# Token mixer and channel mixer on one core: the channel mixer's first product in seven block products in the last token group alone, that group's stores on two queues, and the third output block's halves in two PSUM banks

## Chip, core and metric

The kernel runs on one core of a Trainium2 chip. The metric is device time in microseconds (us) of one execution; lower is better. Times come from repeated executions, views of single instructions from one profiled execution. PE is TensorE (the matmul engine), PEld its weight load, DVE is VectorE, ACT is ScalarE, POOL is GpSimd, SP is SyncE, which issues the DMAs. PSUM is the memory that matmuls write, in eight banks of 512 fp32 columns; SBUF is the working memory.

## What is computed

Three layers follow one another: a linear attention over 768 tokens, a gated layer, and a mixer. The change touches only the last two lines of the mixer:

```python
B, S, d_model, d_tok, d_ch = 2, 768, 384, 256, 1536
xt = x.transpose(0, 2, 1)
h  = np.maximum(xt @ w_tok1, 0.0) @ w_tok2
u  = x + h.transpose(0, 2, 1)                    # 1536 tokens x 384
h2 = np.maximum(u @ w_ch1, 0.0) @ w_ch2          # 384 -> 1536 -> 384
return u + h2
```

## The kernel before

**Precision.** Each matrix is held as a high part in the type fp32r and a low part that is what the high one leaves of fp32. A product is three matmuls: high by high, high by low, low by high (`prod`, the lines L270 to L272). Whatever is a right operand must therefore be split: ACT makes the high part, DVE subtracts it for the low part.

**Tiling of the channel mixer.** The method `rest` runs it. The 1536 tokens are three groups (`g` = 0, 1, 2) of 512 tokens, each two halves `ONE` and `TWO` of 256 columns. The hidden width 1536 is six blocks (`k`) of 256, each two half blocks of 128; `n = 6 g + k` counts all 18 blocks. Of the 384 inputs three blocks of 128 exist (`q`), and of the 384 outputs three blocks (`ct`).

**First product, two forms.** In group 0 it is ordinary (`C1`): for each half block (`b`) three products of 512 columns into one PSUM bank, 18 matmuls of 512 columns for a block. ACT writes relu as the high part `h` and a copy `r` of one half, DVE makes the low part and the two sums `ta` and `tb` that the second product wants (`C1a`, `C1b`). In groups 1 and 2 the first two input blocks form a two by two block product that is done in seven block products instead of eight (`C1s`, seven steps `m` = 0 to 6): seven products of 256 columns and two of 512 for the third input block, 21 matmuls of 256 and 6 of 512 columns. It wants sums of the weight's blocks (`sums_of_c1`, `split_c1`) and of the input's blocks, for each group of tokens anew (`sums_of_u`, `split_u`). Its results lie scattered over three banks `x`, `y`, `z` and are put together by DVE additions (L577) into `c1`, `c2`, then go through ACT for relu and high part (`C1r`), DVE for the low part (`C1l`), and DVE for the differences `ta`, `tb` (`C1t`).

**Second product.** It is in seven block products in all groups for the first two output blocks (`C2`, q = 1 to 7); `sums_of_c2` and `split_c2` make its weight sums on POOL and ACT. The third output block is ordinary (`C2d`, once for each half `t`). A C2 or C2d step is issued once for each of the 18 blocks and accumulates over the six `k` of its group in five PSUM banks (`total(g, i)`): bank 3 uses only its half `ONE`, bank 4 holds both halves of the third output block.

**Finish.** After a group's last block its sums are put together with the residual (`residual`, POOL, three a group, into the one output tile `o`), by ten steps (`finish`, m = 0 to 9, on DVE with ACT and POOL) and two `finish_rest` (L702) for the third output block. Six stores of 128 x 256 go out through SP's queue (`store`).

**Order.** Every engine executes its instructions in the order in which the program issues them. The order of the steps is written by hand as one string, `REST`: each letter or digit is one step for its next block. `a` and `b` are C1, `c` and `d` C1a and C1b, `e`, `f`, `t`, `u` the splits of `ta` and `tb`, `g` to `m` the seven steps of C1s, `o` to `s` C1r, C1l and C1t, `1` to `7` C2, `8` and `9` C2d, `A`, `B` sums and splits of the second product's weights, `C`, `D` those of the first's, `E`, `F` those of the input, `G` to `P` finish, `Q`, `S` finish_rest, `R` residual, `z` a check of the fast path's range (its flag is one small matmul) and `Z` the reading of its flag. The eight banks are shared out as five for `total` and three for everything else.

Of the kernel before, what the change touches and what calls it, by code (L numbers as in the profile page):

```python
# [13 lines left out]
ALU = mybir.AluOpType  # L14
# [3 lines left out]
B, H, S, D = 2, 8, 768, 48  # L18
E = H * D
P = 128  # L20
# [3 lines left out]
DCH = 1536  # L24
# [3 lines left out]
G = 2 * P  # L28
ONE, TWO = slice(0, G), slice(G, 2 * G)
# [40 lines left out]


REST = (
# [5 lines left out]


REBIAS = 2.0 ** -112  # L80
# [5 lines left out]
class Dense:  # L86
# [442 lines left out]

    def C1(self, n, b):  # L530

        p = self.mm(2 * G)
        for q in range(3):
            self.prod(p, self.C1w(n, b, q), self.u[0, q], q == 0, q == 2)
        if b == 0:
            self.raw[n] = [self.temp(q) for q in ("r", "ta", "tb")]
            self.hid[n] = []
        r, h, l = self.raw[n][0], self.big("h"), self.big("l")
        act = self.nc.scalar.activation
        act(r[:, b * G:(b + 1) * G], p[:, b * G:(b + 1) * G], AF.Relu)  # L540
        act(h, p, AF.Relu)
        self.hid[n].append((h, l))
        self.raw[n].append(p)
# [91 lines left out]
    def C2(self, n, q):  # L635

        g, k = divmod(n, DCH // G)
        x = self.hid[n]
        w = lambda q: self.C2w(k, 0, 1) if q == 3 else [t[:, q * P:(q + 1) * P] for t in self.ws["s2"][k]]
        i, o, w, x, c = {  # L640
            1: lambda: (0, ONE, self.C2w(k, 0, 0), x[0], ONE), 2: lambda: (2, ONE, self.C2w(k, 1, 0), x[1], ONE),
            3: lambda: (2, TWO, w(3), x[1], TWO), 4: lambda: (3, ONE, self.C2w(k, 1, 1), x[3], TWO),
            5: lambda: (1, ONE, w(0), x[2], ONE), 6: lambda: (0, TWO, w(1), x[3], ONE),
            7: lambda: (1, TWO, w(2), x[2], TWO)}[q]()
        self.prod(self.total(g, i)[:, o], w, [t[:, c] for t in x], k == 0 and q in (1, 2, 4, 5), k == DCH // G - 1)

    def C2d(self, n, t):
        g, k = divmod(n, DCH // G)
        c = slice(t * G, (t + 1) * G)
        for b in range(2):  # L650
            self.prod(self.total(g, 4)[:, c], self.C2w(k, b, 2), [x[:, c] for x in self.hid[n][b]],
                      k == 0 and t == 0 and b == 0, k == DCH // G - 1 and b == 1)

    def residual(self, n):
        g, ct = divmod(n, 3)
# [7 lines left out]
        self.nc.gpsimd.tensor_tensor(o, hi.bitcast(F32), lo.bitcast(F32), op=ALU.add)  # L663

    def store(self, g, ct, t):
        self.nc.sync.dma_start(self.out[ct * P:(ct + 1) * P, (2 * g + t) * G:(2 * g + t + 1) * G], self.o[ct, t])

    def finish(self, g, m):

# [29 lines left out]
            self.store(g, 1, 0)  # L699

    def finish_rest(self, g, t):
        self.nc.vector.tensor_tensor(self.o[2, t], self.acc[g, 4][:, t * G:(t + 1) * G], self.o[2, t], op=ALU.add)  # L702
        self.store(g, 2, t)

    def want_gate(self):
# [25 lines left out]
    def rest(self, sound=None, flag=None, look=None):  # L731

        self.top.close()
        pool = lambda n, bufs: self.ctx.enter_context(self.tc.tile_pool(name=n, bufs=bufs, reuse_waits="tile"))
        self.pbig = pool("big", 8)
        self.pbig.tile([P, BPAD], F32, name="bpad", bufs=1)
        self.ptmp = pool("tmp", 6)
        self.po = pool("o", 1)
        self.banks = [self.ps3]
        self.ws, self.sw, self.raw, self.acc, self.hid = {}, {}, {}, {}, {}  # L740
        n = DCH // G

        later = lambda f, *a: lambda i: f(i + n, *a)
        parts = dict(A=self.sums_of_c2, B=self.split_c2, C=self.sums_of_c1, D=self.split_c1, E=self.sums_of_u,
                     F=self.split_u, a=lambda i: self.C1(i, 0), b=lambda i: self.C1(i, 1), c=self.C1a, d=self.C1b,
                     e=lambda i: self.right_split(i, 0), f=lambda i: self.right_split(i, 1),
                     o=later(self.C1r, 0), p=later(self.C1l, 0), q=later(self.C1r, 1), r=later(self.C1l, 1),
                     s=later(self.C1t), t=later(self.right_split, 0), u=later(self.right_split, 1),
                     R=self.residual, z=lambda i: flag(sound()) if sound else None, Z=lambda i: look() if look else None)
        parts.update({q: later(self.C1s, m) for m, q in enumerate("ghijklm")})  # L750
        parts.update({str(q): lambda i, q=q: self.C2(i, q) for q in range(1, 8)})
        parts.update({q: lambda i, t=t: self.C2d(i, t) for t, q in enumerate("89")})
        parts.update({q: lambda i, m=m: self.finish(i, m) for m, q in enumerate("GHIJKLMNOP")})
        parts.update({q: lambda i, t=t: self.finish_rest(i, t) for t, q in enumerate("QS")})
        count = dict.fromkeys(parts, 0)
        for part in REST.replace(" ", ""):
            parts[part](count[part])
            count[part] += 1
# [3 lines left out]
def fast(tc, ins, out, flag_pool):  # L762
    nc = tc.nc
    with ExitStack() as ctx:
# [7 lines left out]
        with ExitStack() as c1:  # L772
# [71 lines left out]
            def masked(i, o):  # L844
                A[i, o] = t = dn.a2(nm="A").rearrange("p (h c) -> p h c", c=P)
                nc.scalar.activation(t, PA[i][o], AF.Copy)  # L846
                nc.gpsimd.affine_select(out=t, in_=t, pattern=[[0, NHP], [1, P]],  # L847
                                        compare_op=ALU.is_gt, fill=0.0, base=0,
                                        channel_multiplier=-1)
# [126 lines left out]
            def ahead(f, n):  # L976
                return lambda i: f(i + n) if i + n < N else None
# [7 lines left out]
            def fetch_rest():  # L985
# [4 lines left out]
            parts = dict(  # L990
                L=ahead(load, 2), N=ahead(load_nat, 2), F=ahead(fwd, 1), K=ahead(decay, 1),
                U=ahead(rk, 1), q=ruk, A=a0, S=scores, e=lambda i: masked(i, 0),
# [179 lines left out]
```

## Time and profile before

| | us |
|---|---|
| median of 3 runs | 386.79 |
| lowest, highest | 385.39, 388.01 |
| profiled execution | 386.76 |
| its span, first to last instruction | 384.7 |

The profile's page gives busy times of each engine over the span. A view by stages gives them for a stretch, a timeline gives instructions one by one, with the idle time of the engine before them and what ended it in square brackets. A name such as `tl<-tb,th` says what an instruction writes and what it reads. Lines such as L577 are those of the kernel printed above. The channel mixer takes the last part of the span, from about 231 us.

### The profile page before, as it was taken

The numbers are of one execution on the slowest core, as the hardware profiler recorded it, in microseconds if no ns is written. First come the engines' busy times: TensorE is split into PE (matmuls) and PEld (weight loads), VectorE is DVE, ScalarE is ACT, GpSimd is POOL, SyncE is SP. The second block draws the span as 40 slices with busy tenths as digits, with TensorE's granted clock in tenths as the row PEclk, the third lists the DMA queues.
The fourth block names the chain that finished last, engine by engine and source line by source line (L and its number), as shares of the span: only waits on it lengthen the run. The fifth ranks groups of instructions, "written<-read, shape, count | busy, mean of one in ns | idle before, by whom it ended". The sixth has DMA issues, their size and how long they took to land.

```text
span 384.7 us, 8799 instructions
## 1 busy us (share of the span) xinstructions
PE 372.4 (97%) x3413; PEld 336.6 (87%) x3413; DVE 330.8 (86%) x598; ACT 245.3 (64%) x542; POOL 197.5 (51%) x221
## 2 busy tenths in 40 slices
PE   8999999999999999999999999999999998999992
PEld 3577788889999999999999997899999997989992
DVE  5999998889797787896977887997989999989992
ACT  3799778887345986766666686455466574555650
POOL 4325486763552667668569549879713214114101
PEclk9999999999999999999999999999999999999998
DMA  7675375443361061344542520000001000010002
GB/s 239 207 208 181 106 230 155 132 149 115 95 215 45 2 164 51 87 112 124 165 123 87 164 80 0 3 0 0 2 2 65 5 1 15 0 57 27 3 3 91
DMA packets 16451, 33.74 MB, mean 88 GB/s; under 512 B 2448, under 2 KB 6544, under 8 KB 16400
## 3 DMA queue, kind: packets, MB, share of 16 engines
q1 hardware_dynamic: 16400, 33.09, 28.5%
q8 instruction: 29, 0.48, 0.5%
q14 instruction: 22, 0.18, 0.2%
HBM read 30.72 MB, written 2.36 MB: 86 GB/s over the span
## 4 chain that ended last, share of the span: by engine, by line
PE 68%; DVE 19%; ACT 6%; issue 3%; DMA 2%; SPq 1%; POOL 0%; DVEq 0%; ACTq 0%
PE mm L270 19%; PE mm L271 19%; PE mm L272 19%; DVE p L577 4%; DVE tl L567 3%; DVE l L615 2%; PE py L883 2%; PE pa L841 2%; DVE tb L620 2%; DVE ta L620 2%; DMA st<-in_dram 2%; PE py L867 1%; PE mm L826 1%; PE mm L434 1%; PE tr L295 1%
## 5 line engine op out<-in xcount | busy, mean ns | idle before, releaser
L232 DVE SCALAR_TENSOR_TENSOR st<-st 128x384 int32<-128x384 int32 (+1 forms) x50 | 35.3, 706 | 1.7
L230 DVE SCALAR_TENSOR_TENSOR st<-st 128x384 int32<-128x384 int32 (+1 forms) x50 | 32.9, 657 | 2.4 <-ACT st L228 2.4
L847 POOL TENSOR_SCALAR_AFFINE_SELECT A<-A 128x512 f32<-128x512 f32 x24 | 18.3, 770 | 31.4 <-ACT A L846 29.9
L227 ACT ACTIVATE st<-st 128x384 f32<-128x384 f32 (+1 forms) x50 | 25.9, 517 | 10.6 <-DMA st<-in_dram 10.6
L673 POOL TENSOR_TENSOR o<-o,part 128x256 f32<-128x256 f32 x9 | 7.4, 834 | 42.0 <-ACT part L675 29.6
L819 POOL TENSOR_TENSOR rk<-kr 112x512 f32<-112x512 f32 x12 | 20.3, 1689 | 11.5 <-DMA kr<-in_dram 11.5
L228 ACT ACTIVATE st<-st 128x384 int32<-128x384 uint32 (+1 forms) x50 | 25.8, 517 | 0.0
L663 POOL TENSOR_TENSOR o<-uh,ul 128x512 f32<-128x512 f32 x9 | 14.6, 1650 | 19.7 <-DMA out_dram<-o 12.3
L382 ACT ACTIVATE gh<-vs 128x384 fp32r<-128x384 f32 x16 | 8.4, 524 | 24.3 <-POOL vs L380 24.3
L380 POOL TENSOR_TENSOR vs<-vs,uT 128x384 f32<-128x384 f32 x16 | 19.6, 1232 | 7.1 <-DVE vs L378 7.0
L566 ACT ACTIVATE th<-ta 128x512 fp32r<-128x512 f32 x18 | 11.4, 632 | 15.4 <-DVE ta L620 13.3
L270 PE MATMUL mm<-xt,wuh 128*128 128x256 f32 x72 | 20.8, 289 | 0.0
L271 PE MATMUL mm<-xt,wuh 128*128 128x256 f32 x72 | 20.3, 282 | 0.0
L272 PE MATMUL mm<-xt,wul 128*128 128x256 f32 x72 | 20.3, 282 | 0.0
L610 ACT ACTIVATE h<-p 128x512 fp32r<-128x512 f32 x24 | 15.2, 633 | 7.5 <-PE mm L271 5.2
L793 DVE TENSOR_TENSOR_SCAN wf<-wf,scan 112x516 f32<-112x516 f32 x12 | 18.0, 1499 | 1.7 <-DMA wf<-in_dram 1.7
L815 DVE TENSOR_TENSOR kr<-kr,wf 112x1024 f32<-112x1024 f32 x12 | 15.9, 1328 | 2.2 <-POOL rk L819 1.1
L807 DVE TENSOR_TENSOR_SCAN wf<-wf,scan 112x516 f32<-112x516 f32 x12 | 16.7, 1396 | 0.4
L609 ACT ACTIVATE p<-p 128x512 f32<-128x512 f32 x24 | 14.9, 621 | 2.5 <-DVE p L577 2.3
L577 DVE TENSOR_TENSOR p<-mm,sz 128x512 f32<-128x512 f32 (+1 forms) x24 | 13.2, 550 | 3.6 <-ACT p L598 3.2
L615 DVE TENSOR_TENSOR l<-p,h 128x512 fp32r<-128x512 f32 x24 | 16.2, 682 | 0.0
L270 PE MATMUL mm<-woh,gh 128*128 128x384 f32 x48 | 16.2, 337 | 0.0
(298 smaller groups left out, 1558.8 us busy)
## 6 DMA issues: line engine op xcount, KB each, us to landing
st<-in_dram SPq DMA_DIRECT2D x38, 384.0 KB, 3.5
kr<-in_dram SPq DMA_DIRECT2D x12, 448.0 KB, 4.3
st<-in_dram SPq DMA_DIRECT2D x18, 256.0 KB, 4.1
wf<-in_dram SPq DMA_DIRECT2D x12, 227.5 KB, 2.9
vn<-in_dram SPq DMA_DIRECT2D x12, 192.0 KB, 4.8
out_dram<-o SPq DMA_DIRECT2D x18, 128.0 KB, 1.7
bsg<-in_dram SPq DMA_DIRECT2D x2, 192.0 KB, 3.7
ub<-in_dram SPq DMA_DIRECT2D x1, 3.5 KB, 4.9
```

The lines of the kernel that those rows point to most:

```text
L227: nc.scalar.activation(high.bitcast(F32), high.bitcast(F32), AF.Copy, scale=REBIAS)
L228: nc.scalar.activation(low, low.bitcast(U32), AF.Copy, scale=TOP3, bias=FLOOR)
L230: nc.vector.scalar_tensor_tensor(low, high, -2 ** 31, low, op0=ALU.bitwise_and, op1=ALU.bitwise_or)
L232: nc.vector.scalar_tensor_tensor(low, high, 3, low, op0=ALU.logical_shift_left, op1=ALU.bitwise_or)
L270: mm(out, w[0], x[0], start=first, stop=False, skip_group_check=True)
L271: mm(out, w[0], x[1], start=False, stop=False, skip_group_check=True)
L272: mm(out, w[1], x[0], start=False, stop=last, skip_group_check=True)
L380: nc.gpsimd.tensor_tensor(t, t, self.uT[d, h], op=ALU.mult)
L577: add = lambda o, i, j: self.nc.vector.tensor_tensor(o, i, j, op=ALU.add)
L615: self.nc.vector.tensor_tensor(l, self.raw[n][j], h.bitcast(F32), op=ALU.subtract)
L819: nc.gpsimd.tensor_tensor(RK[i][:PR], KR[i][:, 0], KR[i][:, 1], op=ALU.mult)
L847: nc.gpsimd.affine_select(out=t, in_=t, pattern=[[0, NHP], [1, P]], compare_op=ALU.is_gt, fill=0.0, base=0, channel_multiplier=-1)
```

## The change

Group 1's first product takes the ordinary form, as group 0's does; C1s is left to group 2. So `C1` counts 12 blocks and chooses the token group, the steps `g` to `u` start at block 12, and the sums of the input are made once, for group 2. The third output block's half `TWO` moves into bank 4's half `ONE`, and its half `ONE` into the free half of bank 3; the first write of bank 3 in a group is now the one of C2d. In group 2 the stores go by turns to ACT's and SP's queue, the first to ACT. The string `REST` is written anew.

```diff
-    "abAzAc deBacB fAb12d efBaC3 587695 7EbaFc D412d6 38Fe94 c1Ab2d fBa38c 579CRe AD64b1 Bad23f 89cebg 57612d fhAijC "
...
-    "jkl641 2su3m8 9t5oRu 7615p7 q426r3 s41t23 uR5R7G 64IJH8 L8MKQ9 NOP9S")
+    "abAaBc db1Azc 2e3a8A dfBeB9 cfba5d 7c64C1 2Z3857 6eA1f9 4bB23A 8Rde5a bcB796 def412 C3ac57 89f5b6 dR1A4R C23e78 "
+    "6B9ac4 fb15G2 dea763 H89NI8 J9cDbS 4KLPQd f1D2OC 3acb57 def641 E2DF3F acef8b 5de97C D612a3 89M57b 6g4cR4 d123fD "
+    "857Ceh ai61j5 2cf9b3 d746k8 DRlmeg 9Ro41h fqG23p 5i76rs jJ8kl9 tmNIgo hKQijk ul4HLq mg1Spr os895P hi7tOq upjkM2 "
+    "364152 3rslt8 97mghi oqjklm r61p23 Rusoq8 4p9rt5 7ghisj ku6lt4 R123mu 8o957q 64p51r 2s763t 4u12R3 5G76I4 8H8JLM "
+    "9KQ9NP OS")
...
-        p = self.mm(2 * G)
+        p, (g, k) = self.mm(2 * G), divmod(n, DCH // G)
         for q in range(3):
-            self.prod(p, self.C1w(n, b, q), self.u[0, q], q == 0, q == 2)
+            self.prod(p, self.C1w(k, b, q), self.u[g, q], q == 0, q == 2)
...
-        self.prod(self.total(g, i)[:, o], w, [t[:, c] for t in x], k == 0 and q in (1, 2, 4, 5), k == DCH // G - 1)
+        self.prod(self.total(g, i)[:, o], w, [t[:, c] for t in x], k == 0 and q in (1, 2, 5), k == DCH // G - 1)
...
+        o = self.total(g, 3 + t)[:, (TWO, ONE)[t]]
         for b in range(2):
-            self.prod(self.total(g, 4)[:, c], self.C2w(k, b, 2), [x[:, c] for x in self.hid[n][b]],
-                      k == 0 and t == 0 and b == 0, k == DCH // G - 1 and b == 1)
+            self.prod(o, self.C2w(k, b, 2), [x[:, c] for x in self.hid[n][b]],
+                      k == 0 and b == 0, k == DCH // G - 1 and b == 1)
...
-        self.nc.sync.dma_start(self.out[ct * P:(ct + 1) * P, (2 * g + t) * G:(2 * g + t + 1) * G], self.o[ct, t])
+        self.turn = not self.turn
+        e = self.nc.scalar if g == 2 and self.turn else self.nc.sync
+        e.dma_start(self.out[ct * P:(ct + 1) * P, (2 * g + t) * G:(2 * g + t + 1) * G], self.o[ct, t])
...
-        self.nc.vector.tensor_tensor(self.o[2, t], self.acc[g, 4][:, t * G:(t + 1) * G], self.o[2, t], op=ALU.add)
+        self.nc.vector.tensor_tensor(self.o[2, t], self.acc[g, 3 + t][:, (TWO, ONE)[t]], self.o[2, t], op=ALU.add)
...
-        later = lambda f, *a: lambda i: f(i + n, *a)
-        parts = dict(A=self.sums_of_c2, B=self.split_c2, C=self.sums_of_c1, D=self.split_c1, E=self.sums_of_u,
-                     F=self.split_u, a=lambda i: self.C1(i, 0), b=lambda i: self.C1(i, 1), c=self.C1a, d=self.C1b,
+        later = lambda f, *a: lambda i: f(i + 2 * n, *a)
+        parts = dict(A=self.sums_of_c2, B=self.split_c2, C=self.sums_of_c1, D=self.split_c1, E=lambda i: self.sums_of_u(i + 1),
+                     F=lambda i: self.split_u(i + 2), a=lambda i: self.C1(i, 0), b=lambda i: self.C1(i, 1), c=self.C1a, d=self.C1b,
```

## Rows read from the trace of the kernel before

**Rows 1.** The page, part 1: busy us (share of the span) and instructions, by engine

```profile
PE 372.4 (97%) x3413; PEld 336.6 (87%) x3413; DVE 330.8 (86%) x598; ACT 245.3 (64%) x542; POOL 197.5 (51%) x221
```

**Rows 2.** Busy time by stretch: length, engines' busy us (instructions), clock, DMA share, GB/s

```profile
core 0: us, PE busy (x) PEld busy (x) DVE busy (x) ACT busy (x) POOL busy (x), PEclk, DMA share, GB/s
283.00:325.00 42.00, 40.37 (x311) 38.26 (x309) 40.13 (x87) 24.00 (x47) 11.03 (x14) 1.00 0.06 20
325.00:375.00 50.00, 49.19 (x374) 46.14 (x374) 45.85 (x96) 29.43 (x54) 9.62 (x8) 1.00 0.05 17
```

**Rows 3.** Timeline of PE: start, duration, line, operation, out<-in, shape, count

```profile
230.72 0.40 PE L270 MATMUL mm<-uh,c10h 128*128 128x512 f32 x1
...
245.83 0.39 PE L270 MATMUL mm<-uh,c10h 128*128 128x512 f32 x1
...
249.91 0.28 PE L270 MATMUL mm<-th,c20h 128*128 128x256 f32 x1
...
253.80 0.39 PE L270 MATMUL mm<-uh,c10h 128*128 128x512 f32 x1
...
314.22 0.28 PE L270 MATMUL mm<-h,c21h 128*128 128x256 f32 x1
...
319.74 0.47 PE L270 MATMUL mm<-uh,c12h 128*128 128x512 f32 x1
```

**Rows 4.** Waits after 230 us: us in total, times, longest

```profile
PEld mm L271 <- DVE tl L567: 2.3, 3, 1.6
...
PEld mm L270 <- DVE p L577: 1.2, 4, 0.5
```

**Rows 5.** DVE by line and shape after 231 us: busy us, mean ns, idle before

```profile
L577 DVE TENSOR_TENSOR p<-mm,sz 128x512 f32<-128x512 f32 x12 | 8.2, 682 | 0.2
L546 DVE SCALAR_TENSOR_TENSOR l<-mm,h 128x512 fp32r<-128x512 f32 x12 | 8.1, 679 | 0.6 <-PE mm L271 0.6
L620 DVE TENSOR_TENSOR ta<-p 128x256 f32<-128x256 f32 x12 | 5.0, 417 | 0.0
L546 DVE SCALAR_TENSOR_TENSOR ta<-mm,r 128x256 f32<-128x256 f32 x12 | 5.0, 412 | 1.4 <-ACT h L541 1.2 <-ACT r L540 0.3
L513 DVE TENSOR_TENSOR f<-uh,ul 128x512 f32<-128x512 f32 x4 | 2.8, 748 | 0.0
```

**Rows 6.** Timelines of DVE and POOL near 322 us

```profile
320.85 0.42 DVE L620 TENSOR_TENSOR tb<-p,ta 128x256 f32<-128x256 f32 x1
321.30 1.52 DVE L620 TENSOR_TENSOR tb<-p,tb 128x256 f32<-128x256 f32 x1
322.74 1.78 DVE L567 TENSOR_TENSOR tl<-ta,th 128x512 fp32r<-128x512 f32 x1
...
321.22 4.47 POOL L663 TENSOR_TENSOR o<-uh,ul 128x512 f32<-128x512 f32 x3 [12.26 <-DMA out_dram<-o]
```

**Rows 7.** Timelines of ACT and POOL at the channel mixer's start

```profile
233.26 0.59 ACT L541 ACTIVATE h<-mm 128x512 fp32r<-128x512 f32 x1
...
239.00 1.02 POOL L479 TENSOR_TENSOR s2l<-sw,s2h 128x384 fp32r<-128x384 f32 x1
239.97 0.98 POOL L479 TENSOR_TENSOR c20l<-sw,c20h 128x128 fp32r<-128x128 f32 x1
```

**Rows 8.** Timelines of PE, DVE and SP at the end; last row by stretch

```profile
375.58 0.28 PE L272 MATMUL mm<-h,c22l 128*128 128x256 f32 x1
376.47 0.38 PE L270 MATMUL mm<-h,c22h 128*128 128x256 f32 x1 [0.61 <-DVE o L702]
...
376.99 0.42 DVE L672 TENSOR_TENSOR o<-mm,o 128x256 f32<-128x256 f32 x1 [0.25 <-POOL o L673]
378.15 0.42 DVE L702 TENSOR_TENSOR o<-mm,o 128x256 f32<-128x256 f32 x1 [0.74 <-PE mm L272]
...
378.11 1.42 SPq L666 DMA_DIRECT2D out_dram<-o  x1
379.62 0.39 SPq L666 DMA_DIRECT2D out_dram<-o  x1
...
379.62:384.72 5.10, 0.00 (x0) 0.00 (x0) 0.00 (x0) 0.00 (x0) 0.00 (x0) 0.67 0.20 63
```

More of the change, by code (lines that the diff above doesn't have):

```diff
@@ L740, in rest @@
         self.ws, self.sw, self.raw, self.acc, self.hid = {}, {}, {}, {}, {}
+        self.turn = False
         n = DCH // G
-        later = lambda f, *a: lambda i: f(i + n, *a)
-        parts = dict(A=self.sums_of_c2, B=self.split_c2, C=self.sums_of_c1, D=self.split_c1, E=self.sums_of_u,
-                     F=self.split_u, a=lambda i: self.C1(i, 0), b=lambda i: self.C1(i, 1), c=self.C1a, d=self.C1b,
+        later = lambda f, *a: lambda i: f(i + 2 * n, *a)
+        parts = dict(A=self.sums_of_c2, B=self.split_c2, C=self.sums_of_c1, D=self.split_c1, E=lambda i: self.sums_of_u(i + 1),
+                     F=lambda i: self.split_u(i + 2), a=lambda i: self.C1(i, 0), b=lambda i: self.C1(i, 1), c=self.C1a, d=self.C1b,
                      e=lambda i: self.right_split(i, 0), f=lambda i: self.right_split(i, 1),
```

3 rows, old and new, of the table REST are left out of this document.

## The prediction

> **What bounds the kernel now.** The page's busy times come first: TensorE (PE) is busy 97% of the span, VectorE (DVE) 86%, ScalarE (ACT) 64% [rows 1]. A busy PE there is modelled, so I went on to the table by stages of the last part, the channel mixer that the change touches [rows 2]. The reader is to see the DVE column: 40.13 of 42 us about token group 1, 45.85 of 50 about group 2. The granted clock is 1.00 there, so no term of the sum is a clock.
>
> The third view is PE's instructions in order of time, read for start-to-start spacings [rows 3]. In the ordinary form of the first product, 18 matmuls of 512 columns run from 245.83 to 249.91: 4.08 us, 0.2267 each. The 33 of 256 columns behind them end at 253.80, 0.1179 each; 48 others of 256 columns take 314.22 to 319.74, 0.115 each. I take 0.1165 for 256 columns, about the middle, and 0.2267 for 512.
>
> With these I count what PE loses. From the mixer's first matmul (230.72) to the one at 375.58, ahead of a wait near the end [rows 3, 8], lie 144.86 us. The code issues 180 matmuls of 512 columns there (108 in group 0, 6 in each of 12 seven-product blocks) and 833 of 256. At the spacings that is 180 x 0.2267 + 833 x 0.1165 = 40.8 + 97.0 = 137.8 us. So 7.0 us are lost. The table of waits says to whom: PE's weight loads waited 2.3 us for the DVE's `tl` (L567) and 1.2 for its additions (L577), to name the two longest lines [rows 4]; I put about 0.6 to the guard's flag matmul, which needs a DVE result. So PE is the bound, and DVE is late for it in groups 1 and 2.
>
> **PE's work.** Group 1's six blocks change from 6 matmuls of 512 and 21 of 256 columns to 18 of 512. Old: 6 x 0.2267 + 21 x 0.1165 = 3.81 us. New: 4.08. That is +0.27 a block and **+1.6 us** in all; with 0.1179 or 0.115 for the narrow ones it is +1.5 or +1.8. Nothing hides it: it is work of the engine that bounds.
>
> **DVE's work.** By the groups by shape [rows 5] a seven-product block costs DVE two additions of 0.68 and two of half that width, about 0.42 (L577), two `l` of the wide size (L615) and four narrow differences of 0.42 (L620): 1.36 + 0.84 + 1.36 + 1.68 = 5.2 us. The ordinary form costs two of 0.68 and three of 0.41 from L546, and one more of that width from L557: 3.0 us. So 2.2 us a block, 13.2 in group 1. Of the sums of the input one of two sets falls away: two of 0.75 (L513), four narrow ones and two wide splits, 1.5 + 1.7 + 1.4 = 4.6 us. Together **18 us** of DVE work leave a stretch that held 40.13. They are worth only what PE lost to them.
>
> **What PE still loses.** Of the 7.0 us, 0.6 is the flag. Its matmul now stands behind two more first products, so I cost it at nothing: queued work covers it, and 0.6 returns if that is not so. Some 2.3 us is one place, near 322.7, which the DVE and POOL rows explain [rows 6]: a DVE difference took 1.52, where the one before it, of the same width, took 0.42, and the `tl` behind it 1.78, for as long as POOL ran three residual sums (321.22, 4.47 us), and PE waited up to 1.6 for that `tl` [rows 4]. The rest, 4.1 us, lies over two groups of seven-product blocks, 2.0 a group. One such group is left: **2.0 us**. DVE is looser ahead of it, so it could be 0.5; if nothing improves, all 6.4 stay.
>
> The new order adds a wait at the start. Block 0's third piece of the second product now follows four half products and two short pieces: 230.72 + 4 x 2.04 + 2 x 0.35 = 239.6. It needs the split that POOL finished at 240.95, there behind two sets of sums [rows 7]. Now that split stands behind one set, but its ACT part stands behind the second block's relu: PE's third half product ends at 236.9, ACT needs about 1.0 for a relu of 0.59 and a half-size one, then some 0.8 for two copies, and POOL's 1.02 and 0.98 follow: about 240.2 to 240.7. PE waits **0.5 us**, 1.1 at most, and nothing if both POOL sums are quick. Behind the waiting ACT copies stand later relus, and DVE and then PE wait for these; that cover is a whole block of PE work, 8 us.
>
> So PE loses 2.5 where it lost 7.0: **-4.5 us** (ends -6.5 and 0).
>
> **Moves.** The sums and splits of both weight sets keep their number; those for the first product are needed only in group 2 and move into group 1, where DVE has 18 us of room. Each group's finish keeps its ten steps, three of them with POOL additions, and six stores; in group 0 it is spread further, so the next group's residual sums, which share one output tile with the stores, come later. SP has no loads left here, so a store passes only stores. Residual sums have several us of work ahead of their first reader; they cost something only as in [rows 6].
>
> **The end.** After the matmul at 375.58 the next starts at 376.47, released by the finishing addition of the other half of the same bank [rows 8]. With the halves in two banks it follows after 0.115: PE gains 0.8 and ends near 377.2. But DVE then has the addition at 376.99, which waited for POOL; the last one can follow it at 377.33 and end at 377.75 instead of 378.57. The last store was not issued then: SP was held 1.42 us by the store before it (378.11) and issued at 379.62, an issue of 0.39. With three of the six stores on ACT, SP is through with its second by 377.8 and can issue the last at once: 1.8 us earlier. ACT has no work behind its three issues. Behind the last issue 5.10 us pass with all engines idle [rows 8]; I keep them. An issue on ACT is not in this trace; the ends are SP's 0.39 and 1.42, and I take the first, since there is no earlier store of the same queue just ahead of it. If the last issue is held again the gain is 0.7. I take **-1.6 us**.
>
> **Sum.** The profiled execution took 386.76 (span 384.7): +1.6 - 4.5 - 1.6 gives **382.3 us** (span near 380.2). The median before is 386.79, within 0.03 of it, so the forecast is -1.2% on either.
>
> **Rivals.**
> 1. *POOL stops DVE again.* The six residual sums of groups 1 and 2 now fall beside the one seven-product run. If one set of three costs what it cost near 322.7, that is +2.3: 384.6; with both, 386.9. For it speak the two stretched DVE rows [rows 6]; against it that DVE has room at the first set. Chance 0.17. The Trainium skill states the cause as a rule (SBUF — State Buffer, "Who interferes with whom": a VectorE instruction with two SBUF inputs contends with GpSimd reading SBUF); the trace agrees, 1.52 us against 0.42 for such an instruction, and by that rule the change moves the collision and does not remove it.
> 2. *The hold is not SP's.* If the 1.42 us came from the transfers themselves, a second queue shortens nothing: tail -0.7, 383.2 us. For it: the issue behind the held one took 0.39 on the same queue [rows 8], so the queue alone does not make an issue long. Against: it came fifth in a row on one queue. Chance 0.10. The Trainium skill says as much (DMA: Bandwidth & Descriptors, "Issuing engines are not separate DMA queues": all run on the same 16 engines, and only issue time is saved); no row here has two queues.
> 3. *Slower: the chain of the seven-product block lies open.* Group 2's six blocks pass PE to ACT to DVE to PE with three banks. If each waits as long as the longest row, 1.6 us [rows 4], PE loses 9.6 instead of 2.0 there: 389.9. It decides from 1.1 a block, where the whole gain is gone. For it: DVE at 45.85 of 50 in group 2 [rows 2]. Against: twelve such blocks lost 0.5 each on average, with less room. Chance 0.08.
> 4. *Almost nothing is lost*, 0.5 in all: 380.3. Chance 0.08.
>
> **Chances.** My forecast 0.57, by its own terms 381.2 to 383.6. Range 380.3 to 386.0: below it 0.06, above it rival 3 and rival 1 with both sets, about 0.12. About 1% is what a measurement of this kernel tells from no change, so the bounds are 382.9 and 390.7. The forecast sits 0.6 under the first: 0.38 of its 0.57 counts as faster, with rival 4 and a share of rival 2 it is 0.50. Slower needs nearly all of rival 3 and more: 0.05. The same: 0.45.
>
> **What would show it.** Group 1's DVE time should fall by about 18 us and PE have no wait on `tl` there; 72 more matmuls should be 512 wide and 126 fewer 256. The last addition should end within 0.6 us of PE's end, and the last issue start within 0.1 of it. A PE wait on POOL's splits near 240 would show the start's cost; `tl` rows above 1 us in group 2 would show rival 1; a long issue among the last six, rival 2. The prediction is wrong if PE still loses over 5 us before the end, or if the last issue comes over 1 us behind the last addition.

## The result and the profile after

The changed kernel takes 382.32 us (median; 381.58 to 383.57), the kernel before beside it 386.27: ratio 0.989, 95% interval 0.9873 to 0.9907. That is 1.1% faster; the forecast was 382.3.

The profiled execution of the changed kernel took 383.57 us with a span of 381.8. It is the longest of its times: the mixer's first matmul stands at 231.87, where it stood at 230.72 before, though nothing ahead of it was changed. Among the kernels below, those that keep the same code up to there, it lies between 230.44 and 231.87 without order; I count it as scatter and measure from it.

The page of the changed kernel, part 1 (busy us by engine), against [rows 1]:

```profile
PE 371.1 (97%) x3359; PEld 335.0 (88%) x3359; DVE 318.5 (83%) x566; ACT 234.4 (61%) x528; POOL 195.0 (51%) x221
```

PE has 54 matmuls fewer (72 more of 512 columns, 126 fewer of 256), DVE is busy 12 us less.

The stretches of groups 1 and 2 in the changed kernel (length, busy us of PE, PEld, DVE, ACT, POOL, clock), against [rows 2]:

```profile
284.00:326.00 42.00, 42.00 (x278) 38.48 (x277) 35.91 (x77) 18.88 (x44) 12.68 (x14) 1.00 0.06 20
326.00:373.00 47.00, 47.00 (x374) 45.49 (x374) 42.52 (x88) 27.00 (x51) 10.57 (x11) 1.00 0.06 19
```

PE is busy in every us of both. DVE has room in group 1 (35.91 of 42, where it had 40.13), but hardly more than before in group 2: 42.52 of 47 is 90%, 45.85 of 50 was 92%. The waits of PE's weight loads from 231 us to 376 in the changed kernel, all there are, against [rows 4]:

```profile
PEld mm L271 <- DVE tl L567: 0.3, 1, 0.3
PEld mm L270 <- DVE p L577: 0.2, 1, 0.2
```

The end of the changed kernel: timelines of DVE and SP, then the stretch from the matmul ahead of the last twelve to the end and the one behind the last issue; against [rows 8]:

```profile
374.47 0.42 DVE L675 TENSOR_TENSOR o<-mm,o 128x256 f32<-128x256 f32 x1 [0.26 <-POOL o L676]
374.81 0.41 DVE L705 TENSOR_TENSOR o<-mm,o 128x256 f32<-128x256 f32 x1
...
375.36 0.53 SPq L669 DMA_DIRECT2D out_dram<-o  x1
...
372.94:381.80 8.86, 1.64 (x15) 1.44 (x13) 2.03 (x6) 0.00 (x0) 1.42 (x2) 0.81 0.31 99
...
375.36:381.80 6.44, 0.00 (x0) 0.00 (x0) 0.00 (x0) 0.00 (x0) 0.00 (x0) 0.73 0.24 73
```

The last issue comes 0.14 us behind the last addition, and no issue is held: close to what the prediction asked of the end (0.1, and none held). But 6.44 us follow it where 5.10 did before [rows 8], so that the whole stretch is 8.86 against 9.14.

Where the time went, in the two profiled executions: from the mixer's first matmul to the one ahead of the last twelve 144.86 to 141.07, -3.8; from there to the end -0.3; the later start +1.15; outside the span -0.3. Together -3.2, as 386.76 to 383.57.

### The profile page after: what moved, and what is told of

The parts are those of the page before. It is cut to its first block, busy times and chain, and to the rows that moved or that the text cites. A ratio compares the mean times of both kernels' runs of the same rounds, so it can differ in the third digit from the quotient of the medians.

```text
span 381.8 us, 8639 instructions
## 1 busy us (share of the span) xinstructions
PE 371.1 (97%) x3359; PEld 335.0 (88%) x3359; DVE 318.5 (83%) x566; ACT 234.4 (61%) x528; POOL 195.0 (51%) x221
## 5 line engine op out<-in xcount | busy, mean ns | idle before, releaser
L540 ACT ACTIVATE r<-mm 128x256 f32<-128x256 f32 x24 | 9.2, 382 | 32.9 <-PE mm L272 32.9
L823 POOL TENSOR_TENSOR rk<-kr 112x512 f32<-112x512 f32 x12 | 19.4, 1620 | 11.4 <-DMA kr<-in_dram 11.3
L797 DVE TENSOR_TENSOR_SCAN wf<-wf,scan 112x516 f32<-112x516 f32 x12 | 19.1, 1590 | 1.8 <-DMA wf<-in_dram 1.8
L664 POOL TENSOR_TENSOR o<-uh,ul 128x512 f32<-128x512 f32 x9 | 12.2, 1371 | 14.7 <-DMA out_dram<-o 14.7
L546 DVE SCALAR_TENSOR_TENSOR l<-mm,h 128x512 fp32r<-128x512 f32 x24 | 16.3, 680 | 3.4 <-PE mm L271 3.4
L541 ACT ACTIVATE h<-mm 128x512 fp32r<-128x512 f32 x24 | 14.3, 595 | 6.8 <-PE mm L271 6.8
L811 DVE TENSOR_TENSOR_SCAN wf<-wf,scan 112x516 f32<-112x516 f32 x12 | 17.9, 1490 | 0.4
L567 DVE TENSOR_TENSOR tl<-tb,th 128x512 fp32r<-128x512 f32 x18 | 16.0, 890 | 2.0 <-ACT th L566 1.9
L138 PE MATMUL mm<-scan 112*128 112x512 bf16 x49 | 14.4, 436 | 3.1 <-DVE scan L938 1.6
```

What stands on the lines that cost most here:

```text
L797: nc.vector.tensor_tensor_scan(WF[i][:, WCOL + 2:], WF[i][:, :NHP * CW], scan1.rearrange("p h c -> p (h c)"), 0.0, op0=ALU.mult, op1=ALU.add)
L811: nc.vector.tensor_tensor_scan(r, r, scan2.rearrange("p h c -> p (h c)")[:, ::-1], 0.0, op0=ALU.mult, op1=ALU.add)
L823: nc.gpsimd.tensor_tensor(RK[i][:PR], KR[i][:, 0], KR[i][:, 1], op=ALU.mult)
```

## Experiments on the middle group

**1. The collision in the kernel before, taken away.**

```diff
-        self.nc.gpsimd.tensor_tensor(o, hi.bitcast(F32), lo.bitcast(F32), op=ALU.add)
+        if g == 1:
+            self.nc.gpsimd.memset(o, 0.0)
+        else:
+            self.nc.gpsimd.tensor_tensor(o, hi.bitcast(F32), lo.bitcast(F32), op=ALU.add)
```

> The kernel before, with POOL's three residual sums of the middle group (321.22, 4.47 us) replaced by writing zeros into the same tiles: POOL then reads nothing there, and DVE, ACT and PE keep their work. The output lacks the residual input of the middle group. By the prediction's step these sums stop DVE (1.52 us for an instruction that takes 0.42, and 1.78 for the `tl` behind it) and PE waits 1.6 to 2.3 us for that: the wait should vanish here and the time fall by 1.5 to 2.3 us, to 384.2 to 385.0, with the `tl` near 322.7 back at 0.7. Rival: DVE is late there by its own queue (45.85 of 50 us busy), and the sums only happen to lie beside it: the wait stays over 1 us and the time at 386.0 to 386.5.

Measured: 384.46 us against 386.49, ratio 0.9947 (0.9932 to 0.9963), -2.0. Timelines of DVE and POOL in that kernel, the same instructions as [rows 6]:

```profile
321.82 0.42 DVE L620 TENSOR_TENSOR tb<-p,ta 128x256 f32<-128x256 f32 x1
322.28 0.42 DVE L620 TENSOR_TENSOR tb<-p,tb 128x256 f32<-128x256 f32 x1
322.62 0.68 DVE L567 TENSOR_TENSOR tl<-ta,th 128x512 fp32r<-128x512 f32 x1
...
322.18 1.46 POOL L664 MEMSET o<- 128x512 f32 x3 [12.26 <-DMA out_dram<-o]
```

The waits of PE's weight loads from 283 us to 325 in that kernel, all there are:

```profile
PEld mm L270 <- DVE p L577: 0.7, 2, 0.5
```

1.52 and 1.78 have become 0.42 and 0.68, though POOL still runs beside them, and the wait of 1.6 for `tl` is gone: it was POOL's reading (or its longer time) that stretched DVE, and that cost 2.0 us. The prediction's 2.3 for this place is right in cause and nearly in size; of the 2.3 us that [rows 4] give for `tl`, only the one wait of 1.6 lies here, the other two (0.7) lie in group 2.

**2. The same collisions in the changed kernel.** The edit is that of 1, with `if g >= 1`.

> The changed kernel, with POOL's six residual sums of the middle and last group replaced by writing zeros into the same tiles. The output lacks the residual input of these two groups. In the profile of the changed kernel DVE's rows beside these sums are still stretched (1.60 us for a `tl` beside the sums at 350.28, 1.13 to 1.19 beside the others), but PE's waits for DVE come to 0.5 us in all. Theory: DVE now has room, so the collisions are there and cost nothing: the stretched rows vanish and the time stays within 0.5 us of 382.3. Rival 1 of the prediction, that they still cost: 380.0 to 381.0.

Measured: 381.98 us, ratio 0.9894 (0.9875 to 0.9913): 0.3 below 382.32, within what can be told apart. First the changed kernel itself near its three sums for group 2, timelines of DVE and POOL:

```profile
349.87 0.42 DVE L620 TENSOR_TENSOR tb<-p,tb 128x256 f32<-128x256 f32 x1
350.21 0.42 DVE L577 TENSOR_TENSOR p<-mm,sz 128x256 f32<-128x256 f32 x1
350.55 1.60 DVE L567 TENSOR_TENSOR tl<-ta,th 128x512 fp32r<-128x512 f32 x1
...
350.28 4.33 POOL L664 TENSOR_TENSOR o<-uh,ul 128x512 f32<-128x512 f32 x3 [10.76 <-DMA out_dram<-o]
```

Then the same `tl` without the reading:

```profile
349.27 0.68 DVE L567 TENSOR_TENSOR tl<-ta,th 128x512 fp32r<-128x512 f32 x1
```

The collision is still there, 1.60 for 0.68, and it costs nothing that the time shows, because no matmul waits for this `tl` (the one wait of 0.3 for a `tl` lies before 284 us). What the change removed is not the collision but its price.

**3. DVE work put back.** Fillers on DVE in each block of group 1: five in the first kernel (one in `C1b`, two behind each of the block's two splits), two in the second (one behind each split).

```diff
...
+    def idle(self, n, t, times):
+        for _ in range(times if n // (DCH // G) == 1 else 0):
+            self.nc.vector.tensor_tensor(t, t, t, op=ALU.max)
...
```

> The changed kernel with five more DVE instructions of 128x512 in each block of the middle token group (each takes the maximum of a tile with itself and writes it back, so the values stay): at about 0.6 to 0.68 us each some 18 to 20 us of DVE work are put back into the group that lost 16, while the first product stays in its new form. By the prediction's step the DVE's load in that group is what PE waited for: the table of waits should show rows of PE on DVE in that group again, 2 to 4.5 us in all, and the time be 384.3 to 386.8. Rival: it is the form of the seven-product block itself, a sum that goes from PE to ACT to DVE and back with three banks, and not how much DVE has to do; then filled-in DVE work that is off that chain costs under 1 us: 382.3 to 383.3.

> As the run with 18 us of DVE work put back into the middle group, which cost 17 us, but with two filling instructions a block in place of five: about 7 to 8 us of DVE work put back. The question is how much of the room that the change made on DVE is needed. If the kernel is faster because DVE has room, and all of it is needed, each us put back costs about one: 389 or more. If the room was larger than needed and the price of the first run came from its last third, as DVE's load passes PE's, this costs 0 to 2 us: 382.3 to 384.3. If the form of the block and not DVE's load mattered: 382.3 to 383.0 and no PE wait on DVE in that group.

Measured: 399.39 us with five (ratio 1.0307, 1.0275 to 1.0338) and 386.37 with two (0.9999, 0.9988 to 1.0011). A filler of 512 columns takes 0.69, so two a block are 12 x 0.69 = 8.3 us, and they cost 4.05: the whole gain of the change. PE's waits on DVE from 284 us to 373 and the stretch of group 1 with two fillers:

```profile
PEld mm L270 <- DVE ta L546: 1.8, 2, 1.1
PEld mm L271 <- DVE tl L571: 1.4, 1, 1.4
PEld mm L270 <- DVE p L582: 0.5, 2, 0.4
...
284.00:326.00 42.00, 39.23 (x248) 35.03 (x247) 38.78 (x82) 17.30 (x39) 11.93 (x13) 1.00 0.06 20
```

The longest waits and the same stretch with five:

```profile
PEld mm L271 <- DVE tl L572: 3.7, 4, 2.4
PEld mm L270 <- DVE ta L546: 3.5, 2, 2.7
...
284.00:326.00 42.00, 36.05 (x216) 31.54 (x214) 38.35 (x79) 15.79 (x37) 9.50 (x12) 0.92 0.06 20
```

The rival (the form of the block, not DVE's load) falls: the form is the new one in both, and the waits on DVE are back. My own numbers fall too. I had put 2 to 4.5 us on five fillers, as the kernel before lost 7.0 with as much DVE work; they cost 17.1. The second kernel was to choose between three prices (nothing to 1.0; 0 to 2; all 7 to 8), and gave 4.05, between the last two. So DVE's work in this order has less slack than its 35.91 of 42 suggests: PE waits for the `ta` of L546, which has to read a bank of the first product before PE may write it again, and PE has only three such banks. That the kernel before bore more DVE work because its string puts it at other places is likely, but no run here shows it. With five fillers the clock adds to the price: it is 0.50 for 10.2 us of the middle (312.0 to 318.8 and 332.5 to 335.9), in which PE is busy for 7.8; by half of these, some 4 of the 17.1 us are the clock's, an estimate.

## Experiments at the end

**4. Both edits of the end in the old order.** The kernel before with the change's lines in `C2`, `C2d`, `store` and `finish_rest`, its string and forms kept.

> The kernel before in its own order and with its own forms of the first product, with the two edits of the end alone (stores of the last group on two queues, halves of the third block in two banks). The prediction puts -1.6 us on these: 384.7 against 386.3, ratio 0.996. By the profile of the changed kernel, where the stretch from the matmul ahead of the last twelve to the end shrank from 9.14 to 8.86 us, they are worth 0.3: 386.0, ratio 0.999. If it is -1.6 here, the end of the profiled execution of the changed kernel was a long one and the prediction's term stands; if it is near 0, the whole gain of the change comes from ahead of the end.

Measured: 389.88 us against 386.47, ratio 1.0086 (1.0055 to 1.0117): slower, which neither expectation held. The longest wait, the timelines of DVE and PE around it, and two stretches:

```profile
PEld mm L270 <- DVE o L705: 3.8, 1, 3.8
...
348.27 0.42 DVE L705 TENSOR_TENSOR o<-mm,o 128x256 f32<-128x256 f32 x1
...
344.84 0.28 PE L272 MATMUL mm<-h,c20l 128*128 128x256 f32 x1
348.74 0.58 PE L270 MATMUL mm<-h,c20h 128*128 128x256 f32 x1 [3.62 <-DVE o L705]
349.12 0.41 PE L271 MATMUL mm<-l,c20h 128*128 128x256 f32 x1
349.34 0.41 PE L272 MATMUL mm<-h,c20l 128*128 128x256 f32 x1
349.55 0.41 PE L270 MATMUL mm<-h,c20h 128*128 128x256 f32 x1
...
344.84:348.70 3.86, 0.28 (x3) 0.08 (x1) 3.78 (x9) 0.00 (x0) 0.38 (x1) 0.98 0.25 82
348.70:351.90 3.20, 3.16 (x15) 3.16 (x16) 0.83 (x2) 2.23 (x5) 0.00 (x0) 0.50 0.12 41
```

The two banks are no edit of the end alone. Before, a group opened four banks at its start and the fifth, bank 3, only with its first C2 step `4`. With the edit its first `C2d` steps `8` and `9` open one bank each, so all five are wanted at once, and the last of them must wait until the group before has been read out. The old string has `8 9 s Q` there: the matmuls at 348.74 are those of `9`, and the addition that they wait for is `Q`, the `finish_rest` behind the differences `s`. The wait is 3.8 us; behind it the granted clock is 0.50, 1.2 instead of 2.4 GHz, for 3.2 us, and 15 matmuls run at 0.213 instead of 0.117: 1.4 us more. The new string has `Q` ahead of the next group's fifth bank at both borders. The prediction's step for the end priced the banks without this link; in the new order it happens to cost nothing. At the end itself the edits bring 0.5 us in the old order (8.62 for the last stretch where it was 9.14); ahead of it this kernel loses 4.5 (149.35 us from the mixer's first matmul to the one ahead of the last twelve, where it was 144.86).

**5. Each edit of the end undone in the changed kernel**, the queue, the bank (in all three groups), both:

```diff
-        e = self.nc.scalar if g == 2 and self.turn else self.nc.sync
+        e = self.nc.sync
```

```diff
...
-        o = self.total(g, 3 + t)[:, (TWO, ONE)[t]]
         for b in range(2):
-            self.prod(o, self.C2w(k, b, 2), [x[:, c] for x in self.hid[n][b]],
-                      k == 0 and b == 0, k == DCH // G - 1 and b == 1)
+            self.prod(self.total(g, 4)[:, c], self.C2w(k, b, 2), [x[:, c] for x in self.hid[n][b]],
+                      k == 0 and t == 0 and b == 0, k == DCH // G - 1 and b == 1)
...
```

> The changed kernel with all six stores of the last group on SP again; all else as changed. By the prediction's step for the end, the two banks alone bring the last addition 0.8 us forward and the second queue brings the last issue about 1.0 more, because SP no longer holds it: so this kernel should take 0.9 to 1.1 us more than the changed one, about 383.3, and a store of SP among the last three should show an issue near 1.4 us again. Rival, from the profile of the changed kernel: its last issue came 1.8 us sooner after the last matmul, as forecast, but 6.44 us passed behind it instead of 5.10, with SP's branch at the end open for 3.9 us instead of 2.76; if what follows the last issue is set by something that runs by its own clock (the branch and its instruction fetches), an issue held for 1.4 us moves the end by 0.4 us or less: 382.3 to 382.7.

> The changed kernel with the halves of the third block's sums of the last group back in one bank; the stores stay on two queues. By the prediction the last six matmuls wait again for the addition that reads the other half (0.8 us, with a row of 0.6 released by a DVE addition), the last addition ends 0.4 to 0.8 us later after the last matmul but one and the time grows by 0.8 us: about 383.1. Rival: the end does not follow the last addition but the branch behind the last issue; the wait is there in the trace, and the time grows by 0.3 us or less, 382.3 to 382.6.

> The changed kernel with both edits of the end undone (six stores on SP, the halves of the third block's sums in one bank), the new order and the new form of the first product kept. By the prediction's term for the end, -1.6 us, it should take 383.9. By the profiles so far the end does not hang on the last issue: from the matmul ahead of the last twelve to the end it was 9.12 us in the kernel before, 8.86 in the changed one, 8.78 and 8.87 with one of the two edits undone, while the last issue came 4.04, 2.42, 2.87 and 2.95 after that matmul. So rival: 382.4 to 382.9, and the same stretch near 9.

Measured: 382.64 us (0.9897, 0.9866 to 0.9928), 382.80 (0.9892, 0.9863 to 0.9922) and 383.03 (0.9893, 0.9866 to 0.9919): each less than 0.75 above the changed kernel, and by the ratios to the kernel before beside each (0.989 for the changed one) only 0.1 to 0.3 us; the forecast -1.6 is not there. One by one these differences are within the intervals. The wait that the bank makes is back as expected, in the kernel with one bank:

```profile
PEld mm L270 <- DVE o L704: 0.7, 1, 0.7
```

The longest issue with one queue, then with one bank on two queues, then with both undone:

```profile
372.82 1.00 SPq L669 DMA_DIRECT2D out_dram<-o  x1
```

```profile
375.08 1.21 SPq L668 DMA_DIRECT2D out_dram<-o  x1
```

```profile
374.13 1.64 SPq L668 DMA_DIRECT2D out_dram<-o  x1
...
371.55:381.10 9.55, 1.92 (x15) 1.53 (x13) 2.12 (x6) 0.00 (x0) 1.45 (x2) 0.71 0.28 89
...
375.87:381.10 5.23, 0.00 (x0) 0.00 (x0) 0.00 (x0) 0.00 (x0) 0.00 (x0) 0.50 0.19 62
```

A second queue does not prevent a hold (1.21), one queue brought 1.00 where I had put 1.4, and a later issue is followed by a shorter rest (5.23). So something else runs by its own clock.

**6. The branch at the end left out**, in the changed kernel, in it with the old end, and in the kernel before:

```diff
-        with tc.If(bad):
-            slow(tc, ins, out, scr)
```

> The changed kernel without the conditional second path at its end: the flag is still worked out, but the branch on it and the path behind it are left out of the program. In the changed kernel each engine passes that branch after its last work, SP last, at 375.93, and goes on 3.9 us later, which is all but the end of the span. Theory: the branch and the instruction fetches that it brings fill the time behind the last issue, and the last store's packets queue behind one of these fetches; without them the stretch behind the last issue is 3 us or less instead of 6.44 (the store's landing of 2.4 us, as in the kernel before, and what the program needs to end): 379 or less. Rival: the stretch is the store's own landing and the end of the program, and the branch lies beside it: 381.8 to 382.3.

> As the changed kernel with both edits of the end undone, and the conditional second path at the end left out of the program too (the flag is worked out, the path behind it is missing). Beside the changed kernel without that path (379.03). If the branch at the end is what hides the gain of the two edits, they are worth here what the prediction put on them: 380.6, +1.6, or at least +1.0. If the last issue is held by the branch's instruction fetches alone, there is nothing left to hold it here and only the bank counts: 379.6 to 379.9. If the edits are worth nothing in themselves: 379.0 to 379.4.

> The kernel before without the conditional second path at its end (the flag is worked out, the path behind it is missing). Its hold of 1.42 us before the last store is put down by the prediction to five stores on one queue, and by rival 2 to the transfers. In the changed kernel's version with six stores on one queue and no branch, no issue took more than 0.41. So theory now: the hold comes from the instruction fetches of the branch, and no issue takes over 0.5 here; the stretch from the matmul ahead of the last twelve to the end falls from 9.12 us to 6.6, as in that version, and the time by 2.5 to 3.4, to 383.1 to 384.0. If it is the queue: an issue of 1.4 us is still there, the stretch is 7.5 or more, and the time 384.5 or more.

Measured: 379.03 us (0.98, 0.9771 to 0.9829), 380.53 (0.9836, 0.981 to 0.9862), 384.71 (0.9951, 0.9936 to 0.9966). First the changed kernel, its DMA queues in the last 10.8 us (packets, MB, share) and SP's waits there:

```profile
q1 hardware_dynamic: 432, 0.39, 11.4%
q10 hardware_dynamic: 432, 0.39, 10.9%
q14 instruction: 8, 0.07, 2.1%
q8 instruction: 2, 0.03, 1.4%
...
SPq L1123 <- SPq L1123: 3.9, 1, 3.9
```

In the kernel before SP's row for its branch is shorter:

```profile
SPq L1119 <- SPq L1119: 2.7, 1, 2.7
```

The changed kernel without the branch, the two stretches of its end:

```profile
371.98:377.70 5.72, 1.63 (x15) 1.44 (x13) 2.01 (x6) 0.00 (x0) 1.42 (x2) 0.82 0.40 134
...
374.38:377.70 3.32, 0.00 (x0) 0.00 (x0) 0.00 (x0) 0.00 (x0) 0.00 (x0) 0.69 0.36 118
```

With the old end, the fifth of six stores on SP's one queue, and the stretch:

```profile
374.65 0.33 SPq L668 DMA_DIRECT2D out_dram<-o  x1
...
372.03:378.60 6.57, 1.96 (x15) 1.55 (x13) 1.81 (x5) 0.00 (x0) 1.47 (x2) 0.92 0.30 101
```

The kernel before without the branch, the same:

```profile
378.87 0.38 SPq L666 DMA_DIRECT2D out_dram<-o  x1
...
376.34:382.80 6.46, 1.96 (x15) 1.55 (x13) 2.02 (x6) 0.00 (x0) 1.43 (x2) 0.88 0.37 123
```

Without the branch six stores pass one queue with no issue over 0.41, where with it the longest took 1.00 to 1.64. So the hold is not the queue's: it comes with the branch. With the branch, packets of the kind "instruction" run among the stores (two of 16,384 bytes and eight of 8,192 in the view above), and SP, ACT and DVE, where they have no work left, stand still for 2.4 to 4.3 us behind their branch in the kernels here. The times of single packets in the traces say which of them. In all five kernels with an issue of 1.00 or more (that of experiment 1 is one), a packet of 16,384 bytes is under way when that issue begins, and the issue ends 0.33 to 0.39 us behind it: in the kernel before the packet runs from 377.56 to 379.14, the issue from 378.11 to 379.53. Not every such meeting holds an issue: another packet of that size ran from 374.56 to 375.49 there, and the issue at 374.99 took 0.33. In the changed kernel one occupied a DMA engine from 376.70 to 378.23, for 1.53 us, and the last packets of the last store begin at 378.23. The Trainium skill has a rule on this (Runtime: NRT & Kernel Launch, "Instruction fetch mechanics"): a taken branch to a page not yet loaded makes the engine fetch that page by DMA before it goes on. The trace agrees: the instruction packets and the engines' waits of 2.4 to 4.3 us stand behind the branch, and the changed kernel without the branch has no such packet in its last 13 us.

The old end's stretch falls from 9.14 and 9.55 to 6.46 and 6.57, the new one's from 8.86 to 5.72. So without the branch the edits of the end are worth 0.85 us by the stretch, all of it the bank's; by the medians 1.5 (380.53 against 379.03), with intervals that overlap. Of the three cases expected, the stretch speaks for the second and the median for the first. The time of the kernel before fell by 1.8 and not by the 2.5 to 3.4 expected: its stretch fell by 2.7, but its mixer started 0.7 later in the profiled execution.

**7. Another division of the stores**, to get SP through its branch early:

```diff
-        self.turn = not self.turn
-        e = self.nc.scalar if g == 2 and self.turn else self.nc.sync
+        self.sent += g == 2
+        e = self.nc.scalar if self.sent > 2 else self.nc.sync
...
```

> The changed kernel with another division of the last group's six stores: the first two on SP, the last four on ACT. SP then passes its branch about 2.3 us earlier, before the engines that end late, and its list of waits behind the branch (some 16 of 0.07 us, 1.0 us in all, which in the changed kernel begins when SP goes on at 379.84) runs while ACT is still in its own branch. Theory: the last thing is then ACT's branch, 2.5 to 3.3 us from about 375.7, and the time falls by 1.0 to 1.6 us: 380.7 to 381.3. Rival: the instruction fetches of all engines pass one after the other, whichever engine is last, or four issues in a row hold ACT as six held SP: 382.0 to 382.8.

Measured: 382.20 us, ratio 0.9875 (0.985 to 0.9901), the rival's case. SP's waits, and the stretch of the end:

```profile
SPq L1123 <- SPq L1123: 6.5, 2, 4.3
...
371.82:380.60 8.78, 1.69 (x15) 1.49 (x13) 1.91 (x5) 0.00 (x0) 1.44 (x2) 0.82 0.28 86
```

SP did reach its branch early and then stood there for 4.3 us, and ACT, which passed it last, for 3.5. The stretch is 8.78, as with the other divisions. None of the kernels that compute everything beats the changed one by more than can be told apart.

The ends side by side, in us; "behind it" is from the last issue to the end, the last column from the matmul ahead of the last twelve to the end:

| end, branch | longest of six issues | last addition to last issue | behind it | last stretch |
|---|---|---|---|---|
| before, with | 1.42 | 1.05 | 5.10 | 9.14 |
| before with both edits of the end, with | 0.40 | 0.35 | 6.10 | 8.62 |
| changed, old end, with | 1.64 | 1.42 | 5.23 | 9.55 |
| changed, one queue, with | 1.00 | 0.72 | 5.91 | 8.78 |
| changed, one bank, with | 1.21 | 0.06 | 5.92 | 8.87 |
| changed, with | 0.53 | 0.14 | 6.44 | 8.86 |
| changed, last four on ACT, with | 0.63 | 0.73 | 5.89 | 8.78 |
| before, without | 0.38 | 0.03 | 3.40 | 6.46 |
| changed, old end, without | 0.41 | 0.11 | 3.52 | 6.57 |
| changed, without | 0.37 | 0.14 | 3.32 | 5.72 |

## Why the prediction was right, and where not

The time came out at 382.32 as forecast, but that it fits so closely is luck. The prediction had a gain of 4.5 us from 386.79; the measured gain is 3.95 from 386.27, the median of the kernel before beside it. Inside the gain two errors go against each other: PE's losses fell by 1.0 more than forecast, and the end gave about 1 less (0.9 to 1.5, by the figure that one takes for it).

- **PE's work, +1.6.** Right by the count at the prediction's spacings. In the changed trace 252 matmuls of 512 columns and 707 others lie in the stretch up to the last twelve: 252 x 0.2267 + 707 x 0.1165 = 139.5 us, against 137.8.
- **What PE still loses, 7.0 to 2.5.** Right in direction, too small in size: the stretch took 141.07, so 1.5 us are lost, and the term is -5.5 instead of -4.5. The wait near 322.7 is gone (experiment 1: 2.0). Of the 2.0 for the one group left, less than 0.5 came: PE's weight loads waited 2.4 us in group 2 before and wait 0.2 there now. "DVE is looser ahead of it" is not the whole reason, since DVE is as full in group 2 as it was, and 1.1 of the 2.4 were waits for finishing additions (L672, L702) that the new string has elsewhere. No run here has the new order without the new form, so how the gain divides between the two is not shown. The flag's matmul still costs about 0.2, not nothing.
- **The new wait at the start, 0.5.** It did not show. POOL's second split ended at 241.01, 9.14 us behind the first matmul where I had 9.5 to 10.0, and the piece that I had waiting for it starts at 241.08, so it was in time by 0.07: PE came 0.3 later than in my sum and POOL 0.4 to 0.9 earlier.
- **DVE's work, -18.** Close: summed by the durations of its instructions from 231 us on, DVE's mixer falls from 151.2 to 135.2 us, -16; its busy time falls by only 12, since neighbours overlap. That it is worth only PE's waits fits what was removed; experiment 3 shows that the reverse sum, from added work to lost time, can't be made from busy shares.
- **The end, -1.6.** This step failed. PE's 0.8 from the two banks, the last addition and the issue close behind it all came as forecast (1.36 us for the last twelve matmuls instead of 2.26). "Behind the last issue 5.10 us pass with all engines idle ...; I keep them" is where it broke: 6.44 passed. The rest of the end belongs to the branch of five engines and its fetches (without them 3.32 follow), and behind a last issue that comes earlier more of it is left (5.10 to 6.44). The term is -0.3 in the profiled executions, and by experiment 5 between -0.1 (ratios) and -0.7 (medians).
- **Rival 1** (POOL stops DVE again): its mechanism is there, 1.60 for 0.68, its price is not (experiment 2). The condition that it lacked is a matmul waiting for that `tl`.
- **Rival 2** (the hold is not SP's): it is nearer to what was found, and at 0.10 the chance was too low. The hold is not the queue's, but neither does it come from the stores' own transfers (0.38 without the branch): it comes with the branch's fetches. Its tail of -0.7 lies nearer to the measured one than -1.6. The row that spoke for it, 0.39 for the issue behind the held one on the same queue [rows 8], should have weighed more than "it came fifth in a row".
- **Rival 3** (the block's chain lies open): no; PE waits 0.5 us for DVE in all. **Rival 4** (0.5 lost): no, 1.5 are.

What stays open: why the rest behind the branch takes 2.4 us for one engine and 3.9 for another, which of the fetches decides the end, why one meeting of fetch and issue holds the issue and another does not, how the gain in group 2 divides between order and DVE's work, and why the mixer's start moves by 1.4 us between kernels that are alike up to there.

## What to carry to other kernels

Where an engine that is not the bound is late, moving a collision can be as good as removing it, if nobody waits at the new place; look for the reader, not for the stretched row. Do not carry a tail "behind the last issue" over as a constant: see first whether it hangs on that issue, by a second trace or by what else runs in it. And a group's first write of a bank waits for the bank's last reader in the group before, so a change of which step opens which bank has to be priced at every group's start and not only at the end.

## What the runs showed of the hardware

- A conditional path that is not taken, at the end of the program, cost 3.3 us (382.32 to 379.03) and 1.8 (386.49 to 384.71): instruction packets of 8,192 and 16,384 bytes share the DMA engines with the last stores, an issue of 0.33 to 0.41 became 1.00 to 1.64 where it was held, and such an issue always ended 0.33 to 0.39 us behind a packet of 16,384 bytes, and engines stood 2.4 to 4.3 us behind the branch.
- Behind one PE wait of 3.6 us the granted clock was 0.50 for 3.2 us; with five fillers it was 0.50 for 6.8 us behind waits of 1.2 and 0.7 close together, and for 3.4 us behind one of 2.2. Waits up to 1.6 us in the kernel before left it at 1.00.
- Put-back DVE work cost 0.49 us for each us at 8.3 us, and about 1.05 for each of the next 12.4 (18 more fillers of 0.69; 13.0 us, some 4 of them the lower clock, an estimate).
- A POOL addition that reads SBUF beside a DVE `tensor_tensor` with two SBUF inputs made 1.52 of 0.42 us and 1.60 to 1.78 of 0.68; a POOL memset of the same tiles beside it left 0.42 and 0.68.
